# Sparse attention ahead of two mixtures on one core: the thresholds on ScalarE, the query scaling on GpSimd, the sums' reciprocals turned by transposes, the tail queries divided in rows and the tail keys multiplied in half-width pairs

## Chip, cores and metric

The kernel runs on one core of one Trainium2 chip. The metric is device time in microseconds (us) of that core. The engines are called by the names of the profile: PE (TensorE matmul), PEld (its weight loads), DVE (VectorE), ACT (ScalarE), POOL (GpSimd) and SP (the engine that issues most DMAs).

## What is computed

```python
def _attn_ref(q, k, v, tau):                 # q, k, v: (4, 8, 576, 64)
    scores = scale * np.matmul(q, k.transpose(0, 1, 3, 2))
    thresh = np.max(scores, axis=-1, keepdims=True) - tau
    scores = np.where(scores >= thresh, scores, -1000000000.0)
    scores = scores - np.max(scores, axis=-1, keepdims=True)
    attn = np.exp(scores)
    attn = attn / (np.sum(attn, axis=-1, keepdims=True) + 1e-09)
    return np.matmul(attn, v)
def _moe_ref(x, w_in, w_out, g_ln):          # x: (2304, 512), d_ff 1024
    h = x @ w_in
    e = np.exp(h - np.max(h, axis=-1, keepdims=True))
    solu = h * (e / (np.sum(e, axis=-1, keepdims=True) + 1e-09))
    mu, var = mean(solu), mean((solu - mean(solu)) ** 2)
    return ((solu - mu) / np.sqrt(var + 1e-06) * g_ln) @ w_out
def _moe2_ref(x, w_in, w_out):               # d_ff 2048
    h = x @ w_in
    return (np.maximum(h, 0.0) + np.log1p(np.exp(-np.abs(h)))) @ w_out
```

The three run one after the other: attention, first mixture, second mixture. Everything is float32; the weights arrive as float64 words.

## The kernel before

**Attention** works on 16 pairs of heads (A and B), p = 0 to 15. The queries and keys of a pair lie transposed: 64 rows of head A or of one part of a product, 1216 columns. `split_pair` (L139) makes from them rounded high parts and low parts: DVE multiplies the queries `qr` by 0.125 (L151), ACT rounds them (`q`, L152), POOL subtracts for the low part (L153), and likewise ACT and POOL make `kh` (L148) and `kl` (L149) of the keys. For the first pair alone DVE does the subtractions.

Each pair has nine score tiles of 128 queries by 576 keys: tiles 0 to 7 are the main queries of A and B in turn, tile 8 holds the last 64 queries (the tail) of both heads, one head in the upper and one in the lower 64 rows. `scores` (L158) issues four matmuls for a tile (eight for tile 8) into one of two PSUM buffers `s`, then

- `nm`, the negated row maximum, on DVE (L183),
- `E` = exp(s + nm) on ACT (L185; `T` for tile 8),
- `thr` = -tau - nm, one number per row, on DVE (L186).

`mask` (L189) comes one tile later: one DVE operation multiplies E by (s >= thr) and also gives the row's sum (L192). A PSUM buffer is free for the next tile after that.

Half 0 of a pair is tiles 0 to 3, half 1 is tiles 4 to 8. `xgroup` and `xT` transpose E on PE, 128 columns at a time (L205, L224), and ACT copies the result to `eT` (L207, L216, L225). The keys' tails of both heads share one chunk (chunk 8). `rinv` (L230) makes the reciprocals of the sums on DVE (L233, L234). `rgroup` (L236) turns them so that they lie along the queries: a matmul of `rinv` broadcast to 64 columns with the identity, 64 output rows for each head (L243, and L245 for the tail queries); ACT copies to `R` (L247). `av` (L249) multiplies by the values on PE: chunk 8 with a full 128-column weight (L256), every other chunk with a 64-column weight per head, so that two matmuls fill the two halves of the output (L259). DVE multiplies the result by `R` (L262), and SP writes it to DRAM (L263). Where a float32 matmul stands once in the program, the trace has it twice.

**Order of the work.** The program is written by slots, one for each score tile (`slot`, L265): the scores of tile s of pair p, the mask of the tile before, and stages of the pair before (half 1) or of this pair (half 0). A scheduler then orders each engine's instructions by their dependencies, ahead of a slot or behind it; each engine executes its list in order. Beside the slots run two streams: from 0.4 steps per slot the conversion of the first mixture's weights (`prep_w1`, `convert`; ACT L77, DVE L78, L79, L81, L113, ACT L84, POOL L85), and with 0.55 steps per slot the first mixture itself on units of 256 tokens (`m1_units`: products L330 and L379, transposes L366), which starts when the first four pairs are through. What is left of the first mixture runs after the attention, beside the conversion of the second mixture's weights; then the second mixture.

Of the kernel before, what the change touches and what calls it, by code (L numbers as in the profile page):

```python
# [34 lines left out]
def tile_attention_solu_softplus(ctx: ExitStack, tc: tile.TileContext, q, k, v, tau, w_in, w_out, g_ln, w2_in, w2_out, out):  # L35
# [100 lines left out]
    def split_pair(p, part):  # L136
# [9 lines left out]
        for c in cs:  # L146
# [3 lines left out]
            if p == 0 or part == 0:  # L150
                dve.tensor_scalar_mul(z["qr"][:, c], z["qr"][:, c], 0.125)  # L151
                act.copy(out=z["q"][:, c], in_=z["qr"][:, c])  # L152
                eng.tensor_tensor(out=z["q"][64:128, c], in0=z["qr"][64:128, c], in1=f(z["q"][64:128, c]), op=ALU.subtract)  # L153
# [3 lines left out]
    def scores(p, s):  # L157
        z = st[p]  # L158
        if s == 0:
# [3 lines left out]
            z["T"] = at.tile([P, 576], F32, tag="T", name=f"T{p}")  # L163
# [5 lines left out]
        else:  # L169
            passes = [(512, 0), (576, 640)]  # L170
            E = z["T"]
# [14 lines left out]
        dve.tensor_tensor(out=thr, in0=ntau, in1=nm, op=ALU.subtract)  # L186
# [10 lines left out]
    def xgroup(p, half, c0):  # L197
        """transposes of key chunks c0, c0+1 (or 8: both heads' tails)"""
# [10 lines left out]
        else:  # L209
            w = 256  # L210
            if half == 1:
                for h in range(2):
                    pe.matmul(bk[64 * h:64 * h + 64, 256:320], z["T"][:, 512:576], ident[:, 64 * h:64 * h + 64], start=True, stop=True)
                w = 320
                z[2, 8] = eT[:, 1, 0:64]
            act.copy(out=eT.rearrange("p c q -> p (c q)")[:, 0:w], in_=bk[:, 0:w])  # L216
            z[half, 8] = eT[:, 0, :]
# [12 lines left out]
    def rinv(p, half):  # L230
# [3 lines left out]
        dve.reciprocal(z["rinv"][:, cols], z["rinv"][:, cols])  # L234

    def rgroup(p, half):  # L236
        z = st[p]
        W = 256 + 64 * half
        bk = bank()
        for h in range(2):  # L240
            for j in range(2):
                c = 4 * half + 2 * j + h
                pe.matmul(bk[64 * h:64 * h + 64, P * j:P * j + P], z["rinv"][:, c:c + 1].to_broadcast([P, 64]), ident, start=True, stop=True)  # L243
            if half:
                pe.matmul(bk[64 * h:64 * h + 64, 256:320], z["rinv"][:, 8:9].to_broadcast([P, 64]), ident[:, 64 * h:64 * h + 64], start=True, stop=True)  # L245
        z["R"] = at.tile([P, 320], F32, tag="R", name=f"R{p}_{half}")
        act.copy(out=z["R"][:, 0:W], in_=bk[:, 0:W])  # L247

    def av(p, half):  # L249
# [3 lines left out]
        for part in range(1 + half):  # L253
            o = o_[:, 256 * part:256 * part + (256, 64)[part]]
            e = lambda c: z[half + part, c]
            pe.matmul(o, z["v"][:, 512:640], e(8), start=True, stop=False)  # L256
            for c in range(4):
                for h in range(2):
                    pe.matmul(o[64 * h:64 * h + 64, :], z["v"][:, 256 * h + 64 * c:256 * h + 64 * c + 64], e(4 * h + c),  # L259
                              start=False, stop=(c == 3))  # L260
        x = at.tile([P, 320], F32, tag="x", name=f"x{p}_{half}", bufs=2)
        dve.tensor_tensor(out=x[:, 0:W], in0=o_, in1=z["R"][:, 0:W], op=ALU.mult)  # L262
        sp.dma_start(out=xs[p // NPAIR][p % NPAIR, :, 256 * half:256 * half + W], in_=x[:, 0:W])  # L263

    def slot(p, s):  # L265
        """attention work of one score tile, with the later stages of earlier ones"""
# [387 lines left out]
```

## Time and profile before

| | |
|---|---|
| three runs | 1050.18, 1053.18, 1053.55 us; median 1053.18 us |
| the profiled execution | span 1052.5 us from its first to its last instruction; no other time of it is given |
| busy in the span | PE 960.8 us, DVE 771.0 us, ACT 583.1 us, POOL 179.7 us |
| first and last score matmul | 10.3 us and 499.6 us |

A row of a group of instructions reads: line, engine, operation, output<-input, the tiles' sizes, count | busy time in us and mean ns of one | idle time of the engine just before them and what ended it. A row of the timeline reads: start in us, duration in us, engine, line, operation, output<-input, sizes, count of merged instructions, and in brackets the idle time before them. A row of a stretch reads: start:end, length, then the busy time and number of instructions of PE, PEld, DVE, ACT and POOL, the clock granted to PE (1.00 is full), the DMA engines' share and GB/s. Matmuls overlap, so that the distance from one start to the next tells what a matmul costs PE, not its duration.

### The profile page before, as it was taken

The numbers are of one execution on the slowest core, as the hardware profiler recorded it, in microseconds if no ns is written. First come the engines' busy times: TensorE is split into PE (matmuls) and PEld (weight loads), VectorE is DVE, ScalarE is ACT, GpSimd is POOL, SyncE is SP. The second block draws the span as 40 slices with busy tenths as digits, with TensorE's granted clock in tenths as the row PEclk, the third lists the DMA queues.
The fourth block names the chain that finished last, engine by engine and source line by source line (L and its number), as shares of the span: only waits on it lengthen the run. The fifth ranks groups of instructions, "written<-read, shape, count | busy, mean of one in ns | idle before, by whom it ended". The sixth has DMA issues, their size and how long they took to land.

```text
span 1052.5 us, 15320 instructions
## 1 busy us (share of the span) xinstructions
PE 960.8 (91%) x5792; PEld 794.1 (75%) x5792; DVE 771.0 (73%) x1492; ACT 583.1 (55%) x1030; POOL 179.7 (17%) x85
## 2 busy tenths in 40 slices
PE   3778879899999999999998789899899899999997
PEld 3556657787788888888887687678688788878896
DVE  6888899877877768767399738986665655665565
ACT  4656556765666666656466536554444444444454
POOL 2332332222202222200033233331000100000000
PEclk9888889999999999999998899999999999999999
DMA  7443333222423234010254422411100200000010
GB/s 225 131 132 103 98 102 93 61 57 72 107 70 88 72 73 117 25 40 17 82 175 146 135 86 91 121 59 34 46 1 1 80 1 1 20 21 1 1 41 20
DMA packets 37848, 74.90 MB, mean 71 GB/s; under 512 B 5008, under 2 KB 23440, under 8 KB 37264
## 3 DMA queue, kind: packets, MB, share of 16 engines
q1 hardware_dynamic: 37456, 73.32, 24.1%
q8 instruction: 45, 0.74, 0.3%
q10 hardware_dynamic: 320, 0.62, 0.3%
q14 instruction: 27, 0.22, 0.1%
HBM read 59.77 MB, written 14.16 MB: 70 GB/s over the span
## 4 chain that ended last, share of the span: by engine, by line
PE 59%; DVE 25%; issue 6%; ACT 6%; DMA 4%; POOL 0%; ACTq 0%; DVEq 0%; SPq 0%
PE y L578 11%; PE h L546 11%; PE w L330 8%; PE s L177 7%; PE w L379 7%; PE w L259 5%; PE w L205 5%; DVE thr L186 4%; PE w L243 2%; DVE t L558 2%; DVE w L557 2%; DVE E L192 2%; DVE u L79 2%; PE w L256 2%; DVE w L564 2%
## 5 line engine op out<-in xcount | busy, mean ns | idle before, releaser
L183 DVE TENSOR_REDUCE nm<-s 128x1 f32<-128x576 f32 x144 | 107.3, 752 | 51.5 <-PE s L177 50.8
L177 PE MATMUL s<-kh,q 128*128 128x288 f32 x320 | 104.6, 342 | 43.2 <-DVE T L192 14.8
L578 PE MATMUL y<-wo2h,gh 128*128 128x512 f32 x288 | 114.1, 396 | 11.1 <-DVE yo L582 6.2
L185 ACT ACTIVATE E<-s,nm 128x576 f32<-128x576 f32 x128 | 94.9, 748 | 48.2 <-DVE nm L183 48.1
L546 PE MATMUL h<-x2h,w2h 128*128 128x512 f32 (+1 forms) x320 | 118.9, 372 | 0.0
L546 PE MATMUL h<-x2l,w2h 128*128 128x512 f32 (+1 forms) x320 | 118.7, 371 | 0.0
L546 PE MATMUL h<-x2h,w2l 128*128 128x512 f32 (+1 forms) x320 | 118.5, 370 | 0.0
L578 PE MATMUL y<-wo2h,gl 128*128 128x512 f32 x288 | 113.2, 395 | 4.7 <-DVE gl L567 4.7
L192 DVE SCALAR_TENSOR_TENSOR E<-s,thr,E 128x576 f32<-128x576 f32 x128 | 103.0, 809 | 15.9 <-ACT E L185 14.5
L578 PE MATMUL y<-wo2l,gh 128*128 128x512 f32 x288 | 112.9, 392 | 0.0
L177 PEld LDWEIGHTS s<-kh,q 128*128 128x128 f32 x320 | 64.4, 201 | 57.2 <-issue 35.2
L559 ACT ACTIVATE w<-w 128x512 f32<-128x512 f32 (+1 forms) x80 | 47.1, 589 | 98.3 <-DVE t L558 98.2
L566 ACT CAST gh<-w 128x512 fp32r<-128x512 f32 (+1 forms) x80 | 46.3, 578 | 90.3 <-DVE w L565 90.1
L177 PE MATMUL s<-kl,q 128*128 128x288 f32 x320 | 95.0, 312 | 0.0
L205 PE MATMUL w<-ident,E 128*128 128x128 f32 x576 | 90.6, 289 | 3.0 <-DVE x L262 2.2
L567 DVE TENSOR_TENSOR gl<-w,gh 128x512 fp32r<-128x512 f32 (+1 forms) x80 | 52.4, 655 | 43.4 <-ACT gh L566 42.7
L379 PE MATMUL w<-lh,wo1h 128*128 128x256 f32 x288 | 84.1, 292 | 0.0
L564 DVE SCALAR_TENSOR_TENSOR w<-h,w 128x512 f32<-128x512 f32 (+1 forms) x80 | 50.9, 637 | 45.3 <-ACT w L559 45.3
L379 PE MATMUL w<-ll,wo1h 128*128 128x256 f32 x288 | 81.7, 284 | 0.0
L379 PE MATMUL w<-lh,wo1l 128*128 128x256 f32 x288 | 81.7, 284 | 0.0
L207 ACT COPY eT<-w 128x512 f32<-128x512 f32 x128 | 72.0, 594 | 14.1 <-PE w L205 13.3
L205 PEld LDWEIGHTS w<-ident,E 128*128 128x128 f32 x576 | 71.3, 147 | 10.1 <-issue 5.4
(107 smaller groups left out, 2219.9 us busy)
## 6 DMA issues: line engine op xcount, KB each, us to landing
kr<-in_k_dram SPq DMA_DIRECT2D x30, 304.0 KB, 4.5
qr<-in_q_dram SPq DMA_DIRECT2D x30, 304.0 KB, 4.6
raw<-in_w_in_dram SPq DMA_DIRECT2D x16, 512.0 KB, 3.6
raw<-in_w_out_dram SPq DMA_DIRECT2D x16, 512.0 KB, 3.4
v<-in_v_dram SPq DMA_DIRECT2D x16, 320.0 KB, 3.2
x2s<-x SPq DMA_DIRECT2D x36, 128.0 KB, 1.7
x2r<-x2s SPq DMA_DIRECT2D x9, 512.0 KB, 3.9
out_dram<-yo SPq DMA_DIRECT2D x18, 256.0 KB, 2.2
```

Of the source, the lines that this page charges most:

```text
L177: pe.matmul(ps[:, nh, 0:288], z["q"][:, qc:qc + P], kk[:, kc + 288 * nh:kc + 288 * nh + 288], start=(j == 0), stop=(j == n - 1))
L183: dve.tensor_reduce(out=nm, in_=sv, axis=AX.XY, op=ALU.max, negate=True)
L185: act.activation(out=Ev, in_=sv, func=AF.Exp, bias=nm, scale=1.0)
L192: dve.scalar_tensor_tensor(out=Ev, in0=sv, scalar=thr, in1=Ev, op0=ALU.is_ge, op1=ALU.mult, accum_out=acc)
L205: pe.transpose(bk[:, 256 * ci + P * j:256 * ci + P * j + P], z["E"][2 * half + j][:, ecol(c):ecol(c) + P], ident)
L207: act.copy(out=eT.rearrange("p c q -> p (c q)"), in_=bk)
L259: pe.matmul(o[64 * h:64 * h + 64, :], z["v"][:, 256 * h + 64 * c:256 * h + 64 * c + 64], e(4 * h + c), start=False, stop=(c == 3))
L330: pe.matmul(ps, x_[:, c, P * t:P * t + P], w_[:, c, 512 * n:512 * n + 512], start=(j == 0), stop=(j == 11))
L379: pe.matmul(o, w_[:, c, P * m:P * m + P], l_[:, c, :], start=(j == 0), stop=(j == 23))
L546: pe.matmul(ps, w_[:, kc, :], x_[:, kc, 0:n], start=(j == 0), stop=(j == 11))
L564: dve.scalar_tensor_tensor(out=w_, in0=ps, scalar=0.0, in1=w_, op0=ALU.max, op1=ALU.add)
L578: pe.matmul(y, g_[:, P * j:P * j + P], w_, start=(c == 0 and i == 0), stop=(c == NC2 - 1 and i == 2))
```

## The change

Thresholds: L186 is an ACT operation (Identity with scale -1 and bias -tau) that stands behind the exponential. Scaling: the product of the queries with 0.125 runs on the engine that does the subtractions, which is POOL for 15 of the 16 pairs. Reciprocals: POOL copies the four reciprocals of a half to 64 columns each (`rb`, 256 columns); PE turns them by two full transposes, and ACT copies them to `x`, in which `av` then multiplies in place. Tail queries: POOL multiplies `T` by its reciprocals row by row before it is transposed (576 columns, and the 64 tail keys a second time into new columns 576 to 640), and the tail columns of `x` are set to one by POOL. Chunk 8 of half 1 is transposed last of its groups, with one full transpose for the tail queries in place of two half-width matmuls. Tail keys: chunk 8 is multiplied in two 64-column matmuls as the other chunks are.

```diff
             if p == 0 or part == 0:
-                dve.tensor_scalar_mul(z["qr"][:, c], z["qr"][:, c], 0.125)
+                eng.tensor_scalar_mul(z["qr"][:, c], z["qr"][:, c], 0.125)
...
-        dve.tensor_tensor(out=thr, in0=ntau, in1=nm, op=ALU.subtract)
+        act.activation(out=thr, in_=nm, func=AF.Identity, bias=ntau, scale=-1.0)
...
             if half == 1:
-                for h in range(2):
-                    pe.matmul(bk[64 * h:64 * h + 64, 256:320], z["T"][:, 512:576], ident[:, 64 * h:64 * h + 64], start=True, stop=True)
+                pe.transpose(bk[:, 256:384], z["T"][:, 512:640], ident)
...
         dve.reciprocal(z["rinv"][:, cols], z["rinv"][:, cols])
+        if half:
+            T, r = z["T"], z["rinv"][:, 8:9]
+            pool.tensor_scalar_mul(T[:, 576:640], T[:, 512:576], r)
+            pool.tensor_scalar_mul(T[:, 0:576], T[:, 0:576], r)
+        z["rb"] = at.tile([P, 4, 64], F32, tag="rb", name=f"rb{p}_{half}")
+        pool.tensor_copy(out=z["rb"], in_=z["rinv"][:, 4 * half:4 * half + 4].unsqueeze(2).to_broadcast([P, 4, 64]))
 
     def rgroup(p, half):
-        for h in range(2):
-            for j in range(2):
-                c = 4 * half + 2 * j + h
-                pe.matmul(bk[64 * h:64 * h + 64, P * j:P * j + P], z["rinv"][:, c:c + 1].to_broadcast([P, 64]), ident, start=True, stop=True)
-            if half:
-                pe.matmul(bk[64 * h:64 * h + 64, 256:320], z["rinv"][:, 8:9].to_broadcast([P, 64]), ident[:, 64 * h:64 * h + 64], start=True, stop=True)
-        z["R"] = at.tile([P, 320], F32, tag="R", name=f"R{p}_{half}")
-        act.copy(out=z["R"][:, 0:W], in_=bk[:, 0:W])
+        for j in range(2):
+            pe.transpose(bk[:, P * j:P * j + P], z["rb"][:, 2 * j:2 * j + 2, :].rearrange("p a b -> p (a b)"), ident)
+        x = z["x"] = at.tile([P, 320], F32, tag="x", name=f"x{p}_{half}", bufs=2)
+        act.copy(out=x[:, 0:256], in_=bk[:, 0:256])
+        if half:
+            pool.memset(x[:, 256:320], 1.0)
...
-            pe.matmul(o, z["v"][:, 512:640], e(8), start=True, stop=False)
-            for c in range(4):
+            for i, c in enumerate((8, 0, 1, 2, 3)):
                 for h in range(2):
-                    pe.matmul(o[64 * h:64 * h + 64, :], z["v"][:, 256 * h + 64 * c:256 * h + 64 * c + 64], e(4 * h + c),
-                              start=False, stop=(c == 3))
+                    if c == 8:
+                        w_, e = z["v"][:, 512 + 64 * h:576 + 64 * h], z[half + part, 8][h]
+                    else:
+                        w_, e = z["v"][:, 256 * h + 64 * c:256 * h + 64 * c + 64], z[half + part, 4 * h + c]
+                    pe.matmul(o[64 * h:64 * h + 64, :], w_, e, start=(i == 0), stop=(i == 4))
...
             elif s == 1:
-                xgroup(o, 1, 8); xgroup(o, 1, 0); rinv(o, 1)
+                rinv(o, 1); xgroup(o, 1, 0); xgroup(o, 1, 2)
             elif s == 2:
-                xgroup(o, 1, 2); xgroup(o, 1, 4)
+                xgroup(o, 1, 4); xgroup(o, 1, 6)
             elif s == 3:
-                xgroup(o, 1, 6); xT(o); rgroup(o, 1)
+                xgroup(o, 1, 8); xT(o); rgroup(o, 1)
```

The scheduler makes new lists of it. **DVE, start of pair 2** (nm2_0 is the maximum of tile 0 of pair 2, thr2_0 its threshold, E2_0 the exponentials, w1_4 the weights under conversion). Before:

```order
L183 TENSOR_REDUCE nm2_0_606<-s2_0_601 128x1
L186 TENSOR_TENSOR thr1_8_582<-ntau_115,nm1_8_581 128x1
L78 TENSOR_SCALAR w1_4_691<-raw1_4_540 128x1024
L186 TENSOR_TENSOR thr2_0_607<-ntau_115,nm2_0_606 128x1
L192 SCALAR_TENSOR_TENSOR T1_327,sums1_321<-s1_8_572,thr1_8_582,T1_327 128x576
L192 SCALAR_TENSOR_TENSOR E2_0_596,sums2_594<-s2_0_601,thr2_0_607,E2_0_596 128x576
```

Now:

```order
L183 TENSOR_REDUCE nm2_0_607<-s2_0_602 128x1
L192 SCALAR_TENSOR_TENSOR T1_327,sums1_321<-s1_8_573,thr1_8_583,T1_327 128x576
L81 SCALAR_TENSOR_TENSOR w1_4_696<-raw1_4_543,w1_4_696 128x1024
L183 TENSOR_REDUCE nm2_1_642<-s2_1_637 128x1
L192 SCALAR_TENSOR_TENSOR E2_0_597,sums2_595<-s2_0_602,thr2_0_608,E2_0_597 128x576
L234 TENSOR_SCALAR rinv1_322<-sums1_321 128x5
```

The thresholds are gone from DVE's list, and a conversion step (L81) stands where they stood.

**PE, pair 11 between the scores of tiles 3 and 4** (T10, rinv10 and rb10 belong to half 1 of pair 10). Before:

```order
L224 MATMUL w197_3773<-ident_108,T10_3240 128x128 x4
L243 MATMUL w198_3780<-ident_108,rinv10_3235 64x128 x2
L245 MATMUL w198_3780<-ident_108,rinv10_3235 64x64
L243 MATMUL w198_3780<-ident_108,rinv10_3235 64x128 x2
L245 MATMUL w198_3780<-ident_108,rinv10_3235 64x64
L177 MATMUL s11_4_3789<-kh11_3451,q11_3450 128x288
```

Now:

```order
L225 MATMUL w197_3786<-ident_108,T10_3249 128x128 x4
L249 MATMUL w198_3793<-ident_108,rb10_1_3689 128x128 x2
L177 MATMUL s11_4_3799<-kh11_3463,q11_3462 128x288
```

The six half-width matmuls for the reciprocals are two full transposes in the same place.

**POOL, from the low part of pair 3's keys on** (q3 and kl3 are the low parts of pair 3, T1 and rb1_1 belong to half 1 of pair 1, wo1l to the weights). Before:

```order
L149 TENSOR_TENSOR kl3_766<-kr3_626,kh3_765 128x1216
L85 TENSOR_TENSOR w1l_92<-w1_3_543,w1h_91 128x1024
L153 TENSOR_TENSOR q3_764<-qr3_625,q3_764 64x1216
L85 TENSOR_TENSOR wo1l_94<-w1_4_691,wo1h_93 128x1024
L149 TENSOR_TENSOR kl4_1046<-kr4_904,kh4_1045 128x1216
```

Now:

```order
L151 TENSOR_SCALAR qr3_626<-qr3_626 128x1216
L149 TENSOR_TENSOR kl3_770<-kr3_627,kh3_769 128x1216
L153 TENSOR_TENSOR q3_768<-qr3_626,q3_768 64x1216
L239 TENSOR_SCALAR T1_327<-T1_327,rinv1_322 128x64
L242 COPY rb1_1_652<-rinv1_322 128x256
L240 TENSOR_SCALAR T1_327<-T1_327,rinv1_322 128x576
L85 TENSOR_TENSOR wo1l_94<-w1_4_696,wo1h_93 128x1024
```

The products of T and the copies of the reciprocals stand in POOL's list behind the low parts of the pair after next.

## Rows read from the trace of the kernel before

**Rows 1.** Busy time by stretch: two stretches of the attention.

```profile
10.00:164.00 154.00, 117.97 (x727) 88.59 (x727) 136.52 (x247) 88.24 (x132) 48.82 (x19) 0.87 0.43 125
164.00:502.00 338.00, 328.28 (x2484) 274.86 (x2484) 263.94 (x630) 217.11 (x392) 56.30 (x20) 0.99 0.27 68
```

**Rows 2.** Groups of instructions on DVE from 10 to 164 us.

```profile
L186 DVE TENSOR_TENSOR thr<-ntau,nm 128x1 f32<-128x1 f32 x45 | 34.6, 768 | 0.1
...
L79 DVE SCALAR_TENSOR_TENSOR w<-q,w 128x1024 uint32<-128x1024 uint32 x8 | 10.9, 1361 | 0.0
L81 DVE SCALAR_TENSOR_TENSOR w<-raw,w 128x1024 uint32<-128x1024 uint32 x8 | 9.7, 1218 | 0.0
...
L151 DVE TENSOR_SCALAR qr<-qr 128x1216 f32<-128x1216 f32 x6 | 4.7, 786 | 0.0
```

**Rows 3.** Line L186 in the whole span: duration in ns, min/median/max.

```profile
L186 DVE TENSOR_TENSOR thr<-ntau,nm x144: 114/154/2789, 12.8 to 500.9; 128x1 f32<-128x1 f32 x144
```

**Rows 4.** Timeline of DVE, start of pair 2.

```profile
75.12 1.87 DVE L186 TENSOR_TENSOR thr<-ntau,nm 128x1 f32<-128x1 f32 x1
...
77.52 2.29 DVE L186 TENSOR_TENSOR thr<-ntau,nm 128x1 f32<-128x1 f32 x1
79.73 0.80 DVE L192 SCALAR_TENSOR_TENSOR T<-s,thr,T 128x576 f32<-128x576 f32 x1
```

**Rows 5.** Timeline of POOL in the same stretch.

```profile
74.22 2.75 POOL L149 TENSOR_TENSOR kl<-kr,kh 128x1216 fp32r<-128x1216 f32 x1 [12.48 <-ACT kh L148]
76.93 2.87 POOL L85 TENSOR_TENSOR w1l<-w,w1h 128x1024 fp32r<-128x1024 f32 x1
```

**Rows 6.** Timeline of PE, start of pair 2.

```profile
80.69 0.58 PE L177 MATMUL s<-kh,q 128*128 128x288 f32 x1 [5.97 <-DVE T L192]
...
81.92 0.48 PE L213 MATMUL w<-ident,T 128*64 128x64 f32 x4
```

**Rows 7.** Timeline of PE, half 1 of pair 6, in pair 7.

```profile
240.19 0.60 PE L205 MATMUL w<-ident,E 128*128 128x128 f32 x4
...
240.62 0.60 PE L224 MATMUL w<-ident,T 128*128 128x128 f32 x4
...
242.12 0.40 PE L177 MATMUL s<-kh,q 128*128 128x288 f32 x1
...
242.76 0.59 PE L256 MATMUL w<-eT,v 128*128 128x256 f32 x2
...
243.28 1.95 PE L259 MATMUL w<-eT,v 128*64 128x256 f32 x16
...
245.16 0.43 PE L256 MATMUL w<-eT,v 128*128 128x64 f32 x2
...
245.53 0.69 PE L259 MATMUL w<-eT_T,v 128*64 128x64 f32 x16
...
246.14 0.38 PE L379 MATMUL w<-lh,wo1h 128*128 128x256 f32 x1
```

**Rows 8.** Timeline of PE, pair 11: L213, and L243 of half 0.

```profile
352.36 0.34 PE L213 MATMUL w<-ident,T 128*64 128x64 f32 x4
352.62 0.66 PE L205 MATMUL w<-ident,E 128*128 128x128 f32 x4
...
372.74 0.66 PE L243 MATMUL w<-ident,rinv 128*64 128x128 f32 x8
373.33 0.50 PE L330 MATMUL w<-w1h,xh 128*128 128x512 f32 x1
```

**Rows 9.** Line L352, the one-number operation on ACT: ns, min/median/max.

```profile
L352 ACT ACTIVATE m_t<-m_t x18: 187/203/219, 180.0 to 613.0; 128x1 f32<-128x1 f32 x18
```

**Rows 10.** Timelines of DVE, POOL and PE, pair 11, half 1 of pair 10.

```profile
349.74 0.19 DVE L234 RECIPROCAL rinv<-rinv 128x5 f32<-128x5 f32 x1
...
349.68 2.79 POOL L153 TENSOR_TENSOR q<-qr,q 64x1216 fp32r<-64x1216 f32 x1
...
358.26 0.60 PE L224 MATMUL w<-ident,T 128*128 128x128 f32 x4
```

More of the change, by code (lines that the diff above doesn't have):

```diff
@@ L162, in scores @@
             z["E"] = [at.tile([P, 1152], F32, tag=f"E{i}", name=f"E{p}_{i}") for i in range(4)]
-            z["T"] = at.tile([P, 576], F32, tag="T", name=f"T{p}")
+            z["T"] = at.tile([P, 640], F32, tag="T", name=f"T{p}")
         ps = psS.tile([P, 2, 512], F32, tag="s", name=f"s{p}_{s}", bufs=2)
@@ L170, in scores @@
             passes = [(512, 0), (576, 640)]
-            E = z["T"]
+            E = z["T"][:, 0:576]
         n = 2 * len(passes)
@@ L211, in xgroup @@
             if half == 1:
-                for h in range(2):
-                    pe.matmul(bk[64 * h:64 * h + 64, 256:320], z["T"][:, 512:576], ident[:, 64 * h:64 * h + 64], start=True, stop=True)
-                w = 320
-                z[2, 8] = eT[:, 1, 0:64]
+                pe.transpose(bk[:, 256:384], z["T"][:, 512:640], ident)
+                w = 384
+                ef = eT.rearrange("p c q -> p (c q)")
+                z[2, 8] = [ef[:, 256 + 64 * h:320 + 64 * h] for h in range(2)]
             act.copy(out=eT.rearrange("p c q -> p (c q)")[:, 0:w], in_=bk[:, 0:w])
-            z[half, 8] = eT[:, 0, :]
+            z[half, 8] = [eT[:, 0, :]] * 2
     def xT(p):
@@ L234, in rinv @@
         dve.reciprocal(z["rinv"][:, cols], z["rinv"][:, cols])
+        if half:
[4 more added lines that the diff above has]
+        pool.tensor_copy(out=z["rb"], in_=z["rinv"][:, 4 * half:4 * half + 4].unsqueeze(2).to_broadcast([P, 4, 64]))
     def rgroup(p, half):
         z = st[p]
-        W = 256 + 64 * half
         bk = bank()
-        for h in range(2):
-            for j in range(2):
-                c = 4 * half + 2 * j + h
-                pe.matmul(bk[64 * h:64 * h + 64, P * j:P * j + P], z["rinv"][:, c:c + 1].to_broadcast([P, 64]), ident, start=True, stop=True)
-            if half:
-                pe.matmul(bk[64 * h:64 * h + 64, 256:320], z["rinv"][:, 8:9].to_broadcast([P, 64]), ident[:, 64 * h:64 * h + 64], start=True, stop=True)
-        z["R"] = at.tile([P, 320], F32, tag="R", name=f"R{p}_{half}")
-        act.copy(out=z["R"][:, 0:W], in_=bk[:, 0:W])
+        for j in range(2):
[4 more added lines that the diff above has]
+            pool.memset(x[:, 256:320], 1.0)
     def av(p, half):
@@ L254, in av @@
             o = o_[:, 256 * part:256 * part + (256, 64)[part]]
-            e = lambda c: z[half + part, c]
-            pe.matmul(o, z["v"][:, 512:640], e(8), start=True, stop=False)
-            for c in range(4):
+            for i, c in enumerate((8, 0, 1, 2, 3)):
                 for h in range(2):
-                    pe.matmul(o[64 * h:64 * h + 64, :], z["v"][:, 256 * h + 64 * c:256 * h + 64 * c + 64], e(4 * h + c),
-                              start=False, stop=(c == 3))
-        x = at.tile([P, 320], F32, tag="x", name=f"x{p}_{half}", bufs=2)
-        dve.tensor_tensor(out=x[:, 0:W], in0=o_, in1=z["R"][:, 0:W], op=ALU.mult)
+                    if c == 8:
[3 more added lines that the diff above has]
+                    pe.matmul(o[64 * h:64 * h + 64, :], w_, e, start=(i == 0), stop=(i == 4))
+        x = z["x"]
+        dve.tensor_tensor(out=x[:, 0:W], in0=o_, in1=x[:, 0:W], op=ALU.mult)
         sp.dma_start(out=xs[p // NPAIR][p % NPAIR, :, 256 * half:256 * half + W], in_=x[:, 0:W])
```

## The prediction, made before the changed kernel was run

> **What bounds the kernel now.** I read the busy time by stretch first. The attention falls into two parts with different bounds [rows 1]. From 10 to 164 us (pairs 0 to 4, before the first mixture joins in) DVE is busy for 136.5 of 154 us, 89%, and PE waits for it. From 164 to 502 us (pairs 5 to 15, eleven pairs) PE is busy for 328.3 of 338 us, 97%, and DVE for only 263.9. So what the change takes from DVE counts in the first part, and what it takes from PE in the second. Behind 502 us none of the changed lines runs but for the end of pair 15, and I take no change there.
>
> Then the groups on DVE in the first part [rows 2]. The 45 thresholds, one number per row each, cost 34.6 us, 768 ns apiece, while over the whole span their median is 154 ns and the longest 2789 ns [rows 3]. The reader is to ask what a threshold waits for inside its own duration. The two timelines tell it [rows 4, 5]: the threshold that starts at 75.12 ends at 76.99, and POOL's subtraction ends at 74.22 + 2.75 = 76.97; the one that starts at 77.52 ends at 79.81, and POOL's next ends at 76.93 + 2.87 = 79.80. A threshold that meets a POOL subtraction stands until that is done, and DVE's list behind it stands too. What hangs on it is in PE's timeline: the mask of T came at 79.73 only, and PE had been idle for 5.97 us when the next scores began [rows 4, 6].
>
> For the second part I read the starts of PE's matmuls, since their durations overlap [rows 7, 8].
>
> **The change part by part.** *PE, per pair.* Four transposes take 240.62 - 240.19 = 0.43 us, 0.108 each [rows 7]. (1) Reciprocals of half 1: the four transposes of T start at 240.62 and are through at 241.05, and the next scores start at 242.12 [rows 7]; the matmuls between cost 1.07 us, two transposes cost 0.22, so 0.85 goes. (2) Half 0: from 372.74 to 373.33, 0.59 us [rows 8], becomes 0.22: 0.37 goes. (3) The tail queries of chunk 8: 352.36 to 352.62, 0.26 us [rows 8], becomes 0.11: 0.15 goes. (4) The product with the values in half 1: from 242.76 to 246.14, 3.38 us [rows 7]. Now it is 20 half-width matmuls of 256 columns at no more than 1.88/16 = 0.118 us (243.28 to 245.16) and 20 of 64 columns at 0.61/16 = 0.038 (245.53 to 246.14): 2.35 + 0.76 = 3.11, and one entry into half width. I price an entry by the first L256, which costs 0.52 us where its 256 columns at the half-width pace are worth 0.47 at most, as 0.05 to 0.1. So 0.17 goes; up to 0.4 if the 1.88 holds a change of width at its end. In half 0 the changes of width are as many as before: nothing. The four parts give 1.54 us; with an entry of up to 0.1 saved at (2) and (3) too, and the larger end of (4), 2.0. I take 1.8, as the entries are there in every such row. Over eleven PE-bound pairs that is **20 us** (17 to 22). The list of PE is otherwise the same in this part of the program, so I look for nothing else there. PE's idle 9.7 us in the stretch [rows 1] may shrink or grow; I leave it.
>
> *DVE in the first part.* The thresholds leave their own price, 45 x 0.154 = 6.9 us, and 34.6 - 6.9 = 27.7 us of standing behind POOL. The scaling leaves 5 x 0.786 = 3.9 us [rows 2]. But POOL's long operations stay, 48.8 us of them [rows 1], and DVE keeps others that can meet them: of two conversion steps of the same form and size L79 takes 1361 ns and L81 1218 [rows 2], a small sign that those stood too, and seldom because a threshold ahead of them had taken the wait. In the new list L81 stands just where the two thresholds of 75 to 80 us stood. Between none of the 27.7 us and all of it I take half, 13.9 us, since about half of the operations that can meet POOL remain (41 conversion steps and sums, where there were 45 thresholds besides).
>
> *POOL's new work* is not in the trace. In columns it is 1216 (scaling), 640 (T), 512 (two copies) and 64 (ones) for a pair, 2432 in all. The nearest rows are its subtractions, 2.75 us for 1216 columns with two inputs [rows 5], 2.3 ns a column; at the other end DVE took 0.79 us for the scaling, 0.65 ns a column [rows 2]. That bounds it by 1.6 and 5.6 us; I take the middle, 3.6, as one input should cost less than two. Five pairs add 18 us to POOL's 48.8. If DVE stands for that as for the rest (13.9 of 48.8), it costs 5 us. DVE's list gets shorter by 6.9 + 3.9 + 13.9 - 5 = 19.7 us. DVE is 89% of this part, so 17.5 us reach the end; PE's own changes add a little at half clock in this part (the granted clock is 0.87): **18 us** in sum.
>
> The rule that speaks against this step is in the Trainium skill, "GPSIMD Engine Reference", section "Key points": GpSimd shares its SBUF interfaces with VectorE and contends with VectorE's instructions that have two SBUF inputs or use both ports. The two ends at 76.97 and 79.80 agree with it. By that rule the waits stay with whatever VectorE does next, and the sum would be 20 us, not 38. The same page, section "Engine selection", calls GpSimd's one-input work roughly line-rate, which at its clock would be, as an estimate, 2.0 us for the 2432 columns, and the sum 40.
>
> *ACT* gets 144 operations of one number. The nearest row is 203 ns [rows 9]: 9.1 us in the first part on 88.2 of 154, 20 us in the second on 217.1 of 338 [rows 1]. Its idle time covers them, and if it didn't, they would add at most these 29 us. The mask now waits for a threshold behind the exponential, 0.2 us later; its place in DVE's list is one tile later, behind other work. The copies to `x` in place of `R` are as many; the SP queue has the same transfers.
>
> *The new wait on POOL.* T's transposes, and all the scores behind them on PE, now wait for T to be multiplied, and the turned reciprocals for the copies. In pair 11 the reciprocals are ready at 349.93; POOL is busy with its subtraction until 352.47; PE reaches the four transposes at 358.26 [rows 10]. That leaves 5.8 us for T and the copy, 896 columns, 0.6 to 2.1 us at the two prices. Hidden in the second part. In the first part there is little slack: T's mask ends at 80.53, and PE takes up the first T matmul at 81.92 [rows 4, 6]. There I count it inside the 11% that I took off.
>
> **Sum.** The profiled span is 1052.5 us, the median of the runs 1053.2, 0.7 more. 1052.5 - 20 - 18 = 1014.5, and with 0.7 the forecast is **1015 us**.
>
> **The rivals.**
> *A, the wait moves whole.* Every wait behind POOL that a threshold took is taken by a conversion step or by the sums, and POOL's new 18 us add their share: the first part wins nothing. For it: L81 in the thresholds' place. Against it: nearly half as many operations meet POOL. Time: 1053 - 20 = 1033. Chance 0.20.
> *B, the waits go.* DVE loses all of 34.6 + 3.9 = 38.5 us and the chain follows; PE wins 22 to 25. Time 1053 - 38 - 24 = 991. Against it: half of POOL's operations are 2.8 us long and must meet something. Chance 0.12.
> *C, slower: PE stands behind POOL.* POOL executes its list in order, and the products of T stand behind the low parts of a later pair, which wait for ACT. If they come late, PE stands with all scores and first-mixture products behind it, once per pair. It starts to cost in the second part beyond the 5.8 us of slack, and it decides from 38/16 = 2.4 us per pair on. In the first part up to 5 us a pair are possible (the 5.97 us that PE stood there for T's mask is the row for it), 25 us; in the second 3 us a pair, 33: 1015 + 58 less what is hidden, some 1065. Against it: in pair 11 POOL would need 8 us for 896 columns. Chance 0.07.
> *D, no change.* Half of C eats the win: 1050 to 1056. Chance 0.04.
> The forecast has 0.57. That a threshold stays on DVE, or the scaling, is excluded by the new lists.
>
> **Numbers.** The forecast's own range is 1003 to 1027 (the bounds of the PE sum, 17 and 22, and between a quarter and three quarters of the waits coming back). For 8 in 10 the range takes in A and reaches towards B: 993 to 1036. What a measurement of this kernel can tell from no change is about 0.3%, 3 us. Faster by more than that are the forecast, A and B: 0.89; the same 0.04; slower 0.07.
>
> **What would show it.** On DVE no L186; on ACT 144 of them at about 0.2 us, each right behind its exponential. On PE, no L243 or L245, and per pair some 1.8 us less between the starts; the stretch of eleven pairs shorter by 17 to 22 us. The first five pairs in about 136 us in place of 154, with L79, L81, L113 and the sums' line longer than before on the mean. It is wrong if PE waits for POOL in front of T's transposes or the turned reciprocals in the second part (C), if the means of the conversion steps grow by as much as the thresholds lost (A), or if they don't grow at all (B).

## The result, and the profile after

The changed kernel takes 1034.86 us (median of four runs, 1034.08 to 1036.83) where the kernel before took 1053.3 beside it: a ratio of 0.9828 with a 95% interval of 0.9809 to 0.9848, 18.4 us less. The forecast was 38 us less, 1015. The direction held. The size was a little under half, and the time lies above the forecast's own range (1003 to 1027) and only within the wide one (993 to 1036). The nearest case by its time was rival A with 1033, though for reasons that are only partly A's. The profiled execution spans 1033.4 us.

I measure the two parts by the starts of score matmuls: pair 5 starts at 161.7 us (163.9 before), and from there to the last score matmul it is 323.0 us (335.6). So the first part gave 2.2 us for the 18 forecast, and the second 12.6 for 20. Behind the last score it is 548.7 us (552.9): 4.2 us, where the forecast had nothing.

Busy time by stretch of the changed kernel, the same two parts and the same columns as [rows 1]:

```profile
10.00:162.00 152.00, 103.98 (x654) 79.51 (x655) 121.17 (x196) 94.65 (x175) 84.13 (x46) 0.84 0.45 127
162.00:487.00 325.00, 307.96 (x2355) 264.16 (x2355) 254.06 (x521) 235.11 (x494) 120.91 (x84) 0.99 0.27 70
```

In the first part DVE is busy 121.2 us where it was 136.5, but of 152 us that is 80%: nearly all that came off its work came back as idle time. In the second part PE's busy time fell from 328.3 to 308.0, 20.3 us, while its idle time rose from 9.7 to 17.0. POOL has 84.1 us in place of 48.8, and 120.9 in place of 56.3. What it does, by groups over the whole span:

```profile
L151 POOL TENSOR_SCALAR qr<-qr 128x1216 f32<-128x1216 f32 x15 | 52.4, 3492 | 30.4 <-DMA qr<-in_q_dram 30.4
L149 POOL TENSOR_TENSOR kl<-kr,kh 128x1216 fp32r<-128x1216 f32 x15 | 43.2, 2882 | 76.0 <-ACT kh L148 75.8
...
L240 POOL TENSOR_SCALAR T<-T,rinv 128x576 f32<-128x576 f32 x16 | 27.8, 1734 | 0.0
...
L242 POOL COPY rb<-rinv 128x256 f32<-128x256 f32 x32 | 13.1, 410 | 51.2 <-DVE rinv L235 28.0 <-PE w L267 11.6 <-PE s L177 8.2
...
L239 POOL TENSOR_SCALAR T<-T,rinv 128x64 f32<-128x64 f32 x16 | 8.2, 515 | 25.3 <-DVE rinv L235 24.0 <-DVE m_t L357 1.3
L253 POOL MEMSET x<- 128x64 f32 x16 | 3.0, 186 | 26.4 <-DMA xs<-x 24.4 <-ACT h L339 2.0
```

The new work is 3.49 + 1.73 + 2 x 0.41 + 0.52 + 0.19 = 6.7 us a pair by these means, and 6.4 by the medians of the same rows. The scaling, with one input, takes longer than the subtraction with two. PE's waits from 10 to 162 us (line waited at, releaser: us in total, times, longest) show where that lands:

```profile
PE w L213 <- POOL T L240: 20.3, 4, 7.7
PE s L177 <- DVE E L192: 17.3, 9, 3.6
```

The first row is a wait that the kernel before did not have: the transposes of `T`, with all scores behind them, stand for POOL's product. Pair 2 shows how. DVE's timeline, then POOL's, then PE's, answering to [rows 4 to 6]:

```profile
71.32 2.56 DVE L79 SCALAR_TENSOR_TENSOR w<-q,w 128x1024 uint32<-128x1024 uint32 x1
...
75.20 2.38 DVE L81 SCALAR_TENSOR_TENSOR w<-raw,w 128x1024 uint32<-128x1024 uint32 x1
...
78.91 1.34 DVE L234 TENSOR_SCALAR rinv<-sums 128x5 f32<-128x5 f32 x1
```

```profile
69.42 3.73 POOL L151 TENSOR_SCALAR qr<-qr 128x1216 f32<-128x1216 f32 x1
73.12 3.38 POOL L149 TENSOR_TENSOR kl<-kr,kh 128x1216 fp32r<-128x1216 f32 x1
77.22 3.00 POOL L153 TENSOR_TENSOR q<-qr,q 64x1216 fp32r<-64x1216 f32 x1 [0.72 <-ACT q L152]
80.91 0.50 POOL L239 TENSOR_SCALAR T<-T,rinv 128x64 f32<-128x64 f32 x1 [0.69 <-DVE rinv L235]
81.35 0.39 POOL L242 COPY rb<-rinv 128x256 f32<-128x256 f32 x1
81.73 1.89 POOL L240 TENSOR_SCALAR T<-T,rinv 128x576 f32<-128x576 f32 x1
```

```profile
83.68 0.47 PE L213 MATMUL w<-ident,T 128*128 128x128 f32 x1 [3.25 <-POOL T L240]
```

POOL works without a gap from 69.42 to 76.50. The sums' operation (L234, five numbers per row, 0.15 us where nothing holds it) starts at 78.91 and ends at 80.25, as POOL's subtraction does (77.22 + 3.00 = 80.22): the sums now stand where a threshold stood. Only then come the reciprocal, POOL's 2.7 us for `T`, and PE, which has stood for 3.25 us. So DVE's standing did not vanish, it changed its victim, and behind the new victim hangs a chain to PE.

Pair 2 is one of the four places, and not the longest. Read in the same way, the 20.3 us of all four divide so: 11.4 pass while POOL makes its products and the copy between them; 3.0 pass while the sums stand behind POOL; 2.5 while POOL, with the reciprocals ready, still works at a subtraction (the place of 7.7 us); and 3.4 with the reciprocals and the hand-over between the engines. POOL's own work is thus the largest share.

The groups of DVE from 10 to 162 us, answering to [rows 2]:

```profile
L79 DVE SCALAR_TENSOR_TENSOR w<-q,w 128x1024 uint32<-128x1024 uint32 x8 | 13.2, 1647 | 0.2 <-ACT q L77 0.2
L234 DVE TENSOR_SCALAR rinv<-sums 128x4 f32<-128x4 f32 (+1 forms) x9 | 12.0, 1332 | 0.1
L81 DVE SCALAR_TENSOR_TENSOR w<-raw,w 128x1024 uint32<-128x1024 uint32 x8 | 11.6, 1454 | 0.0
```

For a number of the whole I add up, over DVE's instructions, the duration less the shortest of the same line and form, where that is over 0.1 us. This **standing** was 33.5 us in the first part and 22.5 in the second (28.4 and 16.8 of it in the thresholds). Now it is 22.4 and 30.0, with L234 first in both (10.6 and 14.6). The mechanisms of rivals A (all of it stays) and B (all of it goes) are both excluded by it in the first part: a third went. In the second part the standing grew.

There PE's work for half 1 fell as forecast, the product by more. PE's timeline, half 1 of pair 6, answering to [rows 7]:

```profile
240.28 0.38 PE L249 MATMUL w<-ident,rb 128*128 128x128 f32 x2
240.42 0.38 PE L177 MATMUL s<-kh,q 128*128 128x288 f32 x1
241.13 2.49 PE L267 MATMUL w<-eT,v 128*64 128x256 f32 x24
243.46 0.64 PE L267 MATMUL w<-eT_T,v 128*64 128x64 f32 x16
244.02 0.39 PE L386 MATMUL w<-lh,wo1h 128*128 128x256 f32 x1
```

The reciprocals cost 0.14 us from start to start, and the product 244.02 - 241.13 = 2.89 us where it was 3.38: 0.49 less, for the 0.17 to 0.4 of the forecast.

### The profile page after: what moved, and what is told of

Its sections match the earlier page's. It is cut to its first block, busy times and chain, and to the rows that moved or that the text cites. A ratio compares the mean times of both kernels' runs of the same rounds, so it can differ in the third digit from the quotient of the medians.

```text
span 1033.4 us, 14916 instructions
## 1 busy us (share of the span) xinstructions
PE 926.3 (90%) x5584; PEld 775.2 (75%) x5584; DVE 745.8 (72%) x1333; ACT 607.3 (59%) x1174; POOL 282.0 (27%) x180
## 4 chain that ended last, share of the span: by engine, by line
PE 53%; DVE 24%; ACT 10%; issue 5%; POOL 4%; DMA 4%; SPq 0%; ACTq 0%; DVEq 0%; POOLq 0%
PE y L585 12%; PE h L553 12%; PE w L337 6%; PE s L177 6%; PE w L386 6%; PE w L267 6%; PE w L205 3%; DVE t L565 2%; DVE w L564 2%; DVE u L79 2%; DVE nm L183 2%; DVE E L192 2%; DVE w L571 2%; DVE w L572 2%; DMA qr<-in_q_dram 1%
## 5 line engine op out<-in xcount | busy, mean ns | idle before, releaser
L267 PE MATMUL w<-eT,v 128*64 128x256 f32 (+1 forms) x704 | 94.4, 389 | 3.3 <-ACT eT L217 2.3
L205 PE MATMUL w<-ident,E 128*128 128x128 f32 x576 | 84.1, 281 | 1.7 <-ACT x L389 1.6
L574 DVE TENSOR_TENSOR gl<-w,gh 128x512 fp32r<-128x512 f32 (+1 forms) x80 | 52.4, 655 | 42.9 <-ACT gh L573 42.2
L522 POOL TENSOR_TENSOR x2l<-x2r,x2h 128x1024 fp32r<-128x1024 f32 x9 | 21.5, 2388 | 219.9 <-ACT x2h L521 219.9
```

Source lines behind the costliest of these rows:

```text
L205: pe.transpose(bk[:, 256 * ci + P * j:256 * ci + P * j + P], z["E"][2 * half + j][:, ecol(c):ecol(c) + P], ident)
L267: pe.matmul(o[64 * h:64 * h + 64, :], w_, e, start=(i == 0), stop=(i == 4))
L574: dve.tensor_tensor(out=gl, in0=w_, in1=f(gh), op=ALU.subtract)
```

## The experiments

The theory after the result, **M**: the PE part and the thresholds' move are worth about what was forecast, and POOL's new work takes half of it back, by making DVE stand and by holding `T`. The rival, **N**: the first part is set by something that neither DVE's list nor POOL's moves, so that taking work off POOL gives nothing there. All kernels compute the whole. Pair 5's start and the second part are told as above. Each ratio, and each "less than before", is taken against the kernel before as it ran beside that kernel; its medians were 1052.7 to 1054.9 us.

| kernel | median us | ratio to before (95%) | pair 5 starts | second part | DVE standing, first / second |
|---|---|---|---|---|---|
| before | 1053.3 | 1 | 163.9 | 335.6 | 33.5 / 22.5 |
| after | 1034.9 | 0.983 (0.981 to 0.985) | 161.7 | 323.0 | 22.4 / 30.0 |
| e1 | 1042.6 | 0.991 (0.988 to 0.994) | 149.8 | 336.1 | 23.5 / 19.2 |
| e2 | 1028.4 | 0.977 (0.973 to 0.981) | 155.5 | 321.8 | 21.6 / 20.3 |
| e3 | 1025.9 | 0.974 (0.970 to 0.978) | 152.9 | 325.1 | 27.6 / 21.6 |
| e4 | 1026.2 | 0.974 (0.971 to 0.978) | 153.4 | 324.4 | 21.4 / 18.6 |
| e5 | 1036.7 | 0.984 (0.981 to 0.987) | 148.5 | 331.8 | 16.6 / 21.3 |
| e7 | 1037.2 | 0.985 (0.982 to 0.988) | 164.7 | 325.2 | 27.8 / 29.3 |
| e8 | 1029.5 | 0.977 (0.973 to 0.981) | 151.7 | 322.1 | 18.2 / 22.5 |
| e9 | 1007.7 | 0.957 (0.954 to 0.959) | 149.1 | 310.2 | 3.8 / 0 |
| e10 | 1037.3 | 0.984 (0.980 to 0.988) | 159.1 | 323.8 | 10.8 / 0 |
| e11 | 1016.1 | 0.966 (0.960 to 0.973) | 155.9 | 312.9 | 10.6 / 0 |
| e12 | 1023.7 | 0.971 (0.967 to 0.974) | 156.7 | 315.3 | 9.5 / 1.0 |
| e13 | 1069.0 | 1.013 (1.009 to 1.018) | 168.1 | 346.0 | 36.9 / 42.2 |

**e1, the thresholds alone.** The kernel before with

```diff
-dve.tensor_tensor(out=thr, in0=ntau, in1=nm, op=ALU.subtract)
+act.activation(out=thr, in_=nm, func=AF.Identity, bias=ntau, scale=-1.0)
```

> The kernel before with one part alone: the thresholds on ACT; scaling, reciprocals, tails as before. Theory M (the first part of the attention was to win 18 us and won 2, because POOL's new operations made PE stand for T and DVE's other operations stand behind POOL): without the new work on POOL the thresholds' move pays. The first score of pair 5 comes at 146 to 154 us in place of 163.9, the second part stays as before, time 1036 to 1045 us. Rival N (the length of the first part is set by something that neither DVE nor POOL moves, such as the loads of the weights or the order of the lists): first score of pair 5 at 160 to 165 us, time 1049 to 1055.

The time fell by 10.1 us, as M had it. All of it and more lies in the first part, 14.1 us; the second did not move. DVE's groups from 10 to 150 us show that even so the waits partly found a new place:

```profile
L79 DVE SCALAR_TENSOR_TENSOR w<-q,w 128x1024 uint32<-128x1024 uint32 x8 | 17.7, 2207 | 0.0
```

**e2, e3, e4, POOL relieved.** The changed kernel with the scaling back on DVE (e2), with the products of `T` and the copies `rb` on ACT (e3), with both (e4):

```diff
-eng.tensor_scalar_mul(z["qr"][:, c], z["qr"][:, c], 0.125)
+dve.tensor_scalar_mul(z["qr"][:, c], z["qr"][:, c], 0.125)
...
-pool.tensor_scalar_mul(T[:, 0:576], T[:, 0:576], r)
+act.activation(out=T[:, 0:576], in_=T[:, 0:576], func=AF.Identity, scale=r)
...
-pool.tensor_copy(out=z["rb"], in_=z["rinv"][:, 4 * half:4 * half + 4].unsqueeze(2).to_broadcast([P, 4, 64]))
+act.copy(out=z["rb"], in_=z["rinv"][:, 4 * half:4 * half + 4].unsqueeze(2).to_broadcast([P, 4, 64]))
```

> The changed kernel with the scaling of the queries back on DVE. POOL loses 3.5 us per pair, DVE gets 0.8 back. Theory M: the 20 us that PE stands for T in the first part fall to about 10, the means of L234, L78, L79 fall by half of their excess, first score of pair 5 at 148 to 154 us, time 1021 to 1029 against 1034.9. Rival N: time 1033 to 1038, first score of pair 5 at 160 to 164.

> The changed kernel with the products of T and the copies of the reciprocals on ACT in place of POOL; the scaling stays on POOL. Theory M: PE's wait for T (24.5 us in the span) is gone or under 5 us; DVE's operations still stand behind the scaling, so first score of pair 5 at 147 to 154 us; in the second part 4 us of waits go; time 1018 to 1028. Rival N: time 1033 to 1038.

> The changed kernel with all new work off POOL but the setting to one: scaling on DVE, the products of T and the copies on ACT. Theory M: both wins add up, first score of pair 5 at 140 to 148 us, time 1008 to 1019. Rival N: time 1033 to 1038. If it is no better than the better one of the two single moves, ACT or DVE has become the bound of the first part.

Against the changed kernel e2 is 6.5 us faster and e3 9.0, each mostly in the first part: M, not N. But M missed in three places. In e2 pair 5 starts 1.5 us behind the expected range; in e3 the second part lost nothing (325.1); and e4, which was to take 1008 to 1019 us, gives no more than e3 alone, 8.6 us, so the two prices are not to be added. PE's waits from 10 to 150 us say what remains in e3:

```profile
PE s L177 <- DVE E L192: 30.2, 15, 6.2
...
PE w L213 <- ACT T L240: 1.7, 1, 1.7
```

The wait for `T` is all but gone (20.3 in the changed kernel), and a wait for the masks has grown in its place (17.3 there), with 27.6 us of standing on DVE. It is not shown that the scaling on POOL holds e3 back by that. In e4 the scaling is gone, the standing falls to 21.4 and the wait for the masks to about half:

```profile
PE s L177 <- DVE E L192: 15.9, 11, 3.0
```

Yet pair 5 starts no earlier (153.4); what bounds that part of e4 stays open. In e2 too the standing in the first part hardly moves (21.6 for 22.4). What the scaling's return to DVE took away there is PE's wait for `T`, 5.4 us of 20.3, about as much as the 6.2 us by which pair 5 comes earlier. The same window of e2:

```profile
PE w L213 <- POOL T L240: 14.9, 4, 6.4
```

So the half of M that says "by holding `T`" is borne out in the first part, the half that says "by making DVE stand" is not.

**e5, the thresholds stay on DVE with one SBUF tile read in columns.** The kernel before with

```diff
-dve.tensor_tensor(out=thr, in0=ntau, in1=nm, op=ALU.subtract)
+dve.tensor_scalar(out=thr, in0=nm, scalar1=-1.0, scalar2=ntau, op0=ALU.mult, op1=ALU.add)
```

> The kernel before with the thresholds still on DVE, but as an operation with one SBUF tensor and a number per row (nm times -1 plus -tau) in place of one with two SBUF tensors. Theory M (a threshold stands behind POOL because it reads two SBUF tensors; the other one-number operations of DVE, such as L345 with 146 ns, never stand): the mean of L186 falls from 455 to about 150 ns, the conversions stand longer, first score of pair 5 at 148 to 155 us, time 1036 to 1046. Rival (whatever stands first behind a POOL operation waits): L186 keeps a mean of 400 ns or more, time 1049 to 1055.

```profile
L186 DVE TENSOR_SCALAR thr<-nm,ntau x144: 168/207/216, 12.9 to 481.6; 128x1 f32<-128x1 f32 x144
```

No threshold is longer than 216 ns, where [rows 3] has 2789. At 16.7 us less than before this beats the move to ACT (e1): the operation's form, not its engine, was what stood. In e4's kernel the same form (**e8**) adds nothing that can be told, 1029.5 beside 1026.2 with intervals that overlap. Its time is that of the second case below; its second part, 322.1, lies between the two.

> As e4_pool_free, with the thresholds on DVE as the one-input operation. If masks that wait for a threshold on ACT give back part of PE's win in the second part, it falls from 324.4 to 317 to 321 us, and the time from 1026 to 1018 to 1024. If not, the second part is 323 to 326 us and the time 1024 to 1031, the thresholds' 6.9 us being back on DVE in the first part.

**e7, the PE parts alone.** The changed kernel with the thresholds and the scaling back on DVE; the products of `T` and the copies stay on POOL.

> The changed kernel with thresholds and scaling back on DVE as before: the reciprocals, the tails and POOL's products and copies alone. Theory M: the second part of the attention (first score of pair 5 to the last score, 335.6 us before, 323.0 in the changed kernel) is 321 to 325 us, as this gain comes from PE's matmuls alone; the first part is longer than before, first score of pair 5 at 165 to 173 us, since PE stands for T; time 1040 to 1048. Rival (the thresholds' move is needed for the second part): second part 328 to 334, time 1046 to 1053.

16.2 us less, which is more than M expected (1040 to 1048). The second part is 10.4 shorter, and 7.4 us are saved behind the last score, where of the changed lines only the end of pair 15 runs. The first part is 0.8 longer, with PE waiting for `T`; from 10 to 150 us:

```profile
PE w L213 <- POOL T L240: 10.8, 4, 6.8
```

**e13, the scaling alone on POOL.** The kernel before with that one line changed as in the diff.

> The kernel before with the scaling alone moved to POOL for pairs 1 to 15. DVE loses 0.8 us per pair, POOL gets 3.5 us (measured in the changed kernel) behind which DVE's operations can stand. Theory M: the move costs; the mean of L186 in the whole span rises above its 455 ns, time 1056 to 1064. Rival (as the prediction had it, DVE's list gets shorter and the rest is covered): time 1048 to 1053.

14.7 us slower, more than M expected, and in both parts (4.2 and 10.4). DVE's standing grew by 23 us. The thresholds, untouched, took some 9 of them (10.8 more in the second part, 1.8 less in the first) and the operation of the sums some 5; the rest is spread over other lines. DVE's group of thresholds over the whole span, with 460 ns each in the kernel before:

```profile
L186 DVE TENSOR_TENSOR thr<-ntau,nm 128x1 f32<-128x1 f32 x144 | 74.4, 522 | 0.9
```

**e10, the kernel before without POOL's subtractions.** DVE makes the low parts of all pairs. Nothing on PE is changed.

```diff
-eng = dve if p == 0 else pool
+eng = dve
```

> The kernel before with one edit: the low parts of queries and keys on DVE for all pairs in place of POOL; the thresholds stay as they were, two-input on DVE. DVE gets about 2.5 us of work per pair more. Theory M (what cost the kernel before was POOL's subtractions, behind which DVE stood; the thresholds only took the wait): the mean of L186 in the first part falls from 768 ns to under 350 (only the weights' subtractions are left to stand behind), first score of pair 5 at 145 to 153 us, second part 326 to 332 us, time 1030 to 1041. Rival (DVE is the bound and gets more work): first score of pair 5 at 158 to 168, time 1047 to 1058.

17.6 us less (before took 1054.9 beside it), although DVE's list got 30 operations more of 1.42 us each. The subtraction of the queries on DVE (ns, min/median/max; the two short ones are pair 0's):

```profile
L153 DVE TENSOR_TENSOR q<-qr,q x17: 755/1422/1425, 9.6 to 425.6; 64x1216 fp32r<-64x1216 f32 x15, 64x576 fp32r<-64x576 f32 x1, 64x640 fp32r<-64x640 f32 x1
```

Where the gain lies is not what M expected. The thresholds stand less, as it had it; from 10 to 150 us:

```profile
L186 DVE TENSOR_TENSOR thr<-ntau,nm 128x1 f32<-128x1 f32 x41 | 12.8, 312 | 0.1
```

But pair 5 starts only 4.8 us earlier, at 159.1, in the rival's range (158 to 168) and not in M's (145 to 153): in the first part the longer list of DVE seems to have eaten most of the gain, as the rival said, which is argued and not shown. The gain is in the second part. The stretch from 160 to 480 us:

```profile
160.00:480.00 320.00, 319.43 (x2435) 267.45 (x2434) 260.17 (x642) 213.76 (x386) 0.00 (x0) 1.00 0.27 71
```

The same window of the kernel before:

```profile
160.00:480.00 320.00, 310.28 (x2344) 258.74 (x2343) 251.88 (x593) 206.06 (x368) 57.16 (x20) 0.99 0.28 71
```

With the same matmuls to do, the second part is 11.8 us shorter and PE's idle time falls from 9.7 to 0.6 us. PE's "97% busy" of [rows 1] still held that much of POOL's influence.

**e9, all three parts kept and POOL emptied of attention's large work.** e8 with `eng = dve`, and the scaling folded into the rounding and the subtraction:

```diff
-eng.tensor_scalar_mul(z["qr"][:, c], z["qr"][:, c], 0.125)
-act.copy(out=z["q"][:, c], in_=z["qr"][:, c])
-eng.tensor_tensor(out=z["q"][64:128, c], in0=z["qr"][64:128, c], in1=f(z["q"][64:128, c]), op=ALU.subtract)
+act.activation(out=z["q"][:, c], in_=z["qr"][:, c], func=AF.Identity, scale=0.125)
+dve.scalar_tensor_tensor(out=z["q"][64:128, c], in0=z["qr"][64:128, c], scalar=0.125, in1=f(z["q"][64:128, c]), op0=ALU.mult, op1=ALU.subtract)
```

> As e8, and the low parts of queries and keys on DVE for all pairs, the factor 0.125 inside ACT's rounding and DVE's subtraction: POOL keeps only the weights' subtractions and the setting to one. DVE gets about 1.7 us of work per pair more. Theory M (DVE's standing behind POOL is worth more than the work): first score of pair 5 at 143 to 152 us, second part 316 to 322, time 1010 to 1021. Rival (POOL's work was free and now burdens the bound): first score of pair 5 at 155 to 163, time 1026 to 1036.

1007.7 us, 45.7 less than before, the fastest of all, and faster than M expected (1010 to 1021). Both parts give: 14.8 us in the first, 25.4 in the second. In the first part e5 gave as much (15.4) with one line; it is the second part that sets e9 apart, since no kernel with POOL's subtractions of queries and keys comes under 321.8 there. The folding also takes DVE's scaling away, so that not all of e9's lead over e8 is POOL's. The conversion step L79 is at 1229 ns (1361 before, 1647 after):

```profile
L79 DVE SCALAR_TENSOR_TENSOR w<-q,w 128x1024 uint32<-128x1024 uint32 x8 | 9.8, 1229 | 0.0
```

**e11 and e12, what e9 needs.** e11 is e9 with the products of `T` and the copies on DVE and the two-input thresholds; e12 is the changed kernel with only e9's low parts and folded scaling, so that POOL keeps `T` and `rb`.

> As e9_no_pool, with the products of T and the copies of the reciprocals on DVE in place of ACT and the thresholds as two-input operations on DVE. PE's waits for T and for the copies (13.5 us in the first part of e9) fall to under 6 us, as nothing stands between the reciprocals and the products. Theory M: first score of pair 5 at 143 to 148 us, time 999 to 1006. Rival (DVE's added 1.5 us per pair is on the bound): first score of pair 5 at 149 to 156 us, time 1008 to 1015.

> The changed kernel with thresholds on ACT and the products of T and the copies on POOL as it has them; only the low parts go to DVE and the factor 0.125 into ACT's rounding and DVE's subtraction, as in e9. POOL keeps about 3 us per pair. Theory M (it is POOL's long operations, in front of T in its list and in front of DVE's operations, that ate the gain, not the products of T themselves): PE's wait for T in the first part falls from 20 to under 8 us, first score of pair 5 at 147 to 154, second part 310 to 316, time 1008 to 1018. Rival (T on POOL costs by its own latency): PE's wait for T stays over 12 us, first score of pair 5 at 155 or later, time 1019 or more.

In e9, e11 and e12 the lines behind the subtraction of the queries have numbers lower by one than in the changed kernel. e11 came out as the rival had it, and a little worse (1016.1 for 1008 to 1015): it takes 8.5 us more than e9, 6.8 of it in the first part. Either the work added to DVE makes that, or the two-input thresholds, which stand again behind POOL's subtractions for the weights (DVE's standing there is 6.8 us above e9's); the two were not separated. e12 also came out as the rival had it, by PE's wait for `T`, by pair 5's start (156.7) and by its time; only the second part (315.3) is M's. PE's waits from 10 to 150 us:

```profile
PE w L212 <- POOL T L239: 12.7, 4, 4.8
```

With POOL's long operations on the queries and keys gone, PE still waits 12.7 us for `T` (20.3 in the changed kernel). The trace tells why. At the first of the four places, POOL:

```profile
45.66 1.67 POOL L238 TENSOR_SCALAR T<-T,rinv 128x64 f32<-128x64 f32 x1 [6.34 <-DVE rinv L234]
47.27 0.39 POOL L241 COPY rb<-rinv 128x256 f32<-128x256 f32 x1
47.65 1.72 POOL L239 TENSOR_SCALAR T<-T,rinv 128x576 f32<-128x576 f32 x1
```

POOL had been idle for 6.34 us and started with the reciprocals. At the other three places it had been idle for 1.7 to 8.5 us and started within 0.2 us of the reciprocals too. So no queue is left, and the sums' operation takes 0.16 us at each of the four. Of the 12.7 us, 10.7 pass in POOL's own products and copy, and 2.1 before them. That is the rival's latency; M, by which the products of `T` themselves were not what cost, is wrong here. The first product, 0.45 us where nothing holds it, takes 1.67 here: a two-input subtraction of DVE runs from 45.59 to 47.01, and POOL's product ends 0.3 us behind it, so that POOL too can be the one that stands.

## Why the forecast was twice too large

Two steps failed. The first part's 18 us came out as 2.2, because a new wait of PE for POOL, which I counted "inside the 11%", took 20.3 us. The second part's 20 us came out as 12.6, because PE's idle time there was left at nothing and grew by 7.3. The 4.2 us behind the last score were forecast as nothing; as far as they are unexplained (see below) they are luck.

**PE's term, 20 us: right as work, not as time.** PE's busy time fell by 20.3 us in the stretch; alone (e7) the PE parts shortened it by 10.4 us. The step that failed is "PE's idle 9.7 us in the stretch may shrink or grow; I leave it": it grew by 7.3. PE's waits from 162 to 487 us begin with two that were 0.9 us and nothing in the kernel before, while 3.6 us for the mask of `T` are gone:

```profile
PE s L177 <- DVE E L192: 4.5, 9, 0.9
PE w L213 <- POOL T L240: 4.2, 2, 3.3
```

DVE's standing grew there by 7.5 us, because POOL's scaling meets the first mixture's work too. DVE's timeline in pair 11 has

```profile
352.70 3.88 DVE L351 SCALAR_TENSOR_TENSOR u<-h,u 128x1024 f32<-128x1024 f32 x1
```

while POOL scales from 352.56 to 355.85:

```profile
352.56 3.29 POOL L151 TENSOR_SCALAR qr<-qr 128x1216 f32<-128x1216 f32 x1 [5.56 <-DMA qr<-in_q_dram]
```

e2 and e4 take that growth away (20.3 and 18.6 us), but the second part barely follows (321.8 and 324.4), so the growth of the standing explains little of the idle time. e10 and e9 show more: without POOL's subtractions the part falls to 323.8 with the old matmuls and to 310.2 with the new, 13.6 us apart. PE's busy time is 19.7 us apart there (323.2 and 303.5), close to the 20 of the forecast, and its idle time 6.1 (0.6 and 6.7): even with POOL emptied some of PE's saving comes back as waits. To call the part PE-bound and count DVE and POOL for nothing was the error.

**POOL's price, 3.6 us a pair, bounds 1.6 to 5.6: too low, beyond the upper bound.** It is 6.7, or 6.4 by medians. The step "one input should cost less than two" failed: 3.29 us in the median (3.49 in the mean) for 1216 columns with one input against 2.78 (2.88) with two. The Trainium skill, "GPSIMD Engine Reference", section "Engine selection", has one-input work at roughly line-rate, 2.0 us for a pair as I estimated from it; the trace does not agree.

**DVE's standing in the first part: the net near, by luck.** Forecast was 13.9 us less and 5 more; it fell by 33.5 - 22.4 = 11.1. But the thresholds' move alone (e1) took 10.0 and not 13.9: of the 28.4 us that stood in thresholds about two thirds came back, not half. And POOL's new work added nothing to it (22.4 beside e1's 23.5), where 5 were forecast. L81 and L79 did lengthen. DVE's busy time fell by 15.3 us for 19.7 forecast.

**"There I count it inside the 11%": the step that cost most.** I turned DVE's shorter list into time by its share of 89%, which supposes that no new wait arises. ("At half clock" there is a misreading besides: a granted clock of 0.87 in the mean is nearer to the full one. No number hangs on it.) PE's wait for `T`, 20.3 us in four pieces of up to 7.7, is rival C's mechanism with rival C's price for the first part (25 us), and it arises in the forecast case. I had bounded POOL's slack where there is plenty (5.8 us in pair 11), and had not drawn the chain sums, reciprocal, product of `T`, transposes for pair 2, where [rows 4, 6] left 1.4 us.

**The parts add up in sum, not by stretch.** Thresholds alone 10.1 less (e1), the PE parts alone 16.2 less (e7), the scaling 6.5 more (changed kernel against e2): 19.8 less in sum, measured 18.4. In the first part the same three give 14.1 - 0.8 - 6.2 = 7.1 less where 2.2 were measured, in the second 8.7 where it was 12.6; so the near sum is partly chance. Nor is M's "about what was forecast" right: the thresholds and the PE parts, each alone, give 26.3 of the 38 us. The scaling's price depends on the kernel around it: 14.7 where the thresholds are on DVE (e13).

**ACT's threshold, 203 ns: too low.** It takes 286:

```profile
L186 ACT ACTIVATE thr<-nm,ntau x144: 278/286/364, 13.5 to 486.6; 128x1 f32<-128x1 f32 x144
```

The row I used had no operand per row. The Trainium skill, "ScalarE: Activation LUTs", section "What ACT_TABLE_LOAD costs", gives such an operation some 280 ns, and this trace agrees. The masks waited 20 us in all for these thresholds, 17 of them in the second part.

**Left open.** No kernel starts pair 5 before 148.5 us; what sets that is not shown. DVE's standing does not: e5 has 16.6 us of it and starts pair 5 at 148.5, e9 has 3.8 and starts it at 149.1, e10 has 10.8 and starts it at 159.1. The granted clock differs too, from 0.81 (e12) to 0.90 (e5) between 10 and 148 us, and no kernel holds it fixed. Behind the last score the kernels with the new PE parts take 545.5 to 549.2 us, those with the old ones 552.9 to 555.8. Of that 1.7 us is the end of pair 15 (17.3 us from the last score to its last product, where it was 19.0); behind it the code is the same, and the rest is not explained. And e9 combines ACT for `T` with an emptied POOL; that this is the least is not shown.

## To carry to other kernels

An operation that is far longer at its worst than at its median may be a victim: look for the engine whose instruction ends where it ends. Moving the victim hands part of the wait to the next in line; here it paid about equally to write the victim in another form (e5, 16.7 us) and to take that engine's instructions away (e10, 17.6). Before work is moved to an idle engine, price it by that engine's own rows and draw the chain behind it for the tightest place in the program; here the "free" GpSimd was the dearest engine, and taking its subtractions away (e10) was worth about as much as the whole change (18.4). And the wait for its result counts its own time, not only its queue (e12). A busy share of 97% does not prove a bound: e10 took 12 us from such a stretch without touching that engine's work.

## What was not expected

- Even a DVE operation of four or five numbers per row stands behind POOL: L234, 0.15 us alone, has a mean of 1332 ns in the first part. The one-input threshold of e5 (216 ns at most) does not.
- POOL takes 2.7 to 3.0 ns a column with one input (1216 in 3.29 us, 576 in 1.73), and 2.3 to 2.4 with two, where DVE scales 1216 columns in 0.79.
- The subtraction that POOL does in 2.8 us takes 1.4 on DVE, and moving 30 of them there made the kernel faster by 17.6 us, 11.8 of them in the second part, though DVE seemed the bound of the first.
